# Retention with a gated convolution on one core: the first batch in order of arrival, its queries by chunk, output weights later

## The chip, the core and the metric

The kernel runs on one core of a Trainium2 chip. The metric is the device time of one execution, in microseconds (us), from the first to the last instruction. TensorE (PE) multiplies matrices into PSUM, VectorE (DVE) and ScalarE (ACT) read PSUM and write SBUF, GpSimd (POOL) works on SBUF alone, and SyncE (SP) issues nearly all DMA transfers, in the order of its program. Every engine works through its own list of instructions in order and waits where an instruction needs something that isn't there yet.

## What is computed

Eight batches of 576 tokens go through decayed attention with 8 heads of 64, and the result through a gated block of width 512:

```python
q, k, v: (8, 8, 576, 64) float32        # batch, heads, tokens, head size
scores = scale * q @ k.T                # scale = 1/8
Dmat   = gamma[h] ** (i - j) if i >= j else 0
x      = (scores * Dmat) @ v            # heads side by side: (8, 576, 512)

gate = sigmoid(sum over kk = 0..4 of conv_w[kk] * x[token - 4 + kk])   # causal, per channel
val  = x @ w_val                        # 512 x 512
out  = (gate * val) @ w_out             # 512 x 512, float32
```

There is no softmax. The decay splits into a factor of the query's token (`gout`) and one of the key's token (`gin`), so that only a 0/1 mask stays inside a chunk, and everything before the chunk goes through a state of 64 x 64 for each head, to which each chunk adds k.T @ v.

## The kernel before

Tokens are taken in chunks of 128; batches come in groups of four. Of each group the 16 full chunks come first, and then the last 64 tokens of its batches, two batches to a "tail" chunk: 36 chunks in all, numbered 0 to 35 in this order. Two chunks make a unit, so there are 18 units of convolution, gate, value and output product.

Loads: k and v of a full chunk are 256 KB each, in pieces of 64 floats (256 B). The queries of a batch come as one load of 1 MB, in which a partition takes four neighbouring tokens, so that a piece is 1 KB. The four turns of such a load give queries in an order in which a chunk's columns are interleaved; `mask_q` is the mask in this order, and the convolution's input is written back in the order of tokens.

```python
def load(t):                       # k and v of chunk t, of a tail its q too
    load_one("k", k, kind, b, c, LA + 1)          # LA = 8
    if kind == "tail":
        load_one("q", q, kind, b, c, 2)
    load_one("v", v, kind, b, c, LA + 1)

def load_queries(b):
    t = half.tile([P, H, RQ, D], F32, name="fqb", bufs=2)
    nc.sync.dma_start(out=..., in_=q[b, :, 0:RQ * P, :].rearrange("h (p r) d -> p h (r d)", r=RQ))

load_one("k", k, *chunks[0], LA + 1)
load_queries(0)
load_one("v", v, *chunks[0], LA + 1)
load(1)
...                                # wvf: w_val, one load of 1 MB
load(2)
...                                # wof: w_out, four loads of 64 rows each
load(3)
load_queries(1)
for t in range(4, LA - 2):
    load(t)
```

For each chunk: k, q and v are cast to bf16 (v times `gin`); k and q are transposed on TensorE and copied out of PSUM; scores, the mask, the part carried by the state, the values, the update of the state. The steps of the main loop hold these for several chunks at once:

```python
for t in range(-2, NT + 2):        # NT = 36
    n = t // 2 - 1                 # the unit: convolution and value in an even step, output in the odd one
    ...                            # t == -2: cast and turn chunk 0's k, all of batch 0's q
    for b in qload.get(t, []): load_queries(b)
    load(t + LA - 2)
    cast_v(t + 2); cast_k(t + 3); cast_q(...)
    take_state(t)
    scores(t + 1); masks(t + 1, 0)
    values(t)
    ...
    conv(n); gate(n, 0); gate(n, 1)           # even t
    turn_k(t + 2)
    ...
    project(n, 0) if odd else value(n, 0)
    turn_q(...)
    project(n, 1) if odd else value(n, 1)     # project stores to the output, by SyncE
    carried(t + 1); update(t + 1)
    ...                            # in the first steps: conversion of the weights
```

(Conditions on the range of t are left out.) Each store of the output is an instruction on SyncE, in line with the loads: the stores of unit n come before the load of chunk 2n + 10.

Of the kernel before, what the change touches and what calls it, by code (L numbers as in the profile page):

```python
# [21 lines left out]
def kernel(  # L22
# [48 lines left out]
    with tc.manual_schedule():  # L71
# [13 lines left out]
        def load(t):  # L85
            kind, b, c = chunks[t]
            load_one("k", k, kind, b, c, LA + 1)
            if kind == "tail":
                load_one("q", q, kind, b, c, 2)
            load_one("v", v, kind, b, c, LA + 1)  # L90
# [9 lines left out]
        load_one("k", k, *chunks[0], LA + 1)  # L100
        load_queries(0)
        load_one("v", v, *chunks[0], LA + 1)
        load(1)
        wvf = consts.tile([P, NP, DM], F32, name="wvf")
        wof = consts.tile([P, NP, DM], F32, name="wof")
        nc.sync.dma_start(out=wvf, in_=moe_w_val.rearrange("(o i) n -> i o n", i=P))
        load(2)
        wo_src = moe_w_out.rearrange("(pr ab hl p) n -> ab hl p pr n", pr=2, ab=2, hl=2)
        for (p0, blk, ab, hl) in ((0, 0, 0, 0), (64, 0, 1, 0), (0, 2, 1, 1), (64, 2, 0, 1)):
            nc.sync.dma_start(out=wof[p0:p0 + 64, blk:blk + 2, :], in_=wo_src[ab, hl])  # L110
        load(3)
        load_queries(1)
        for t in range(4, LA - 2):
            load(t)


        lrow = consts.tile([P, H], F32, name="lrow")
# [33 lines left out]
        for pr in range(NP):  # L151
            nc.scalar.activation(gout[:, pr, :], posi, AF.Exp, bias=lsc, scale=lcol[:, pr:pr + 1])

        sbd = [consts.tile([P, NP, P], BF16, name=f"sbd{i}") for i in range(2)]
        sbl = [consts.tile([P, NP, P], BF16, name=f"sbl{i}") for i in range(GB)]
        xg = [xp.tile([P, GB, NP, PAD + S], BF16, name=f"xg{g}") for g in range(B // GB)]
        for t in sbd:
            nc.vector.memset(t, 0.0)
# [30 lines left out]
        def prep_wo(copy, o):  # L189
            copy(wob[:, o], wof[:, o])  # L190
# [4 lines left out]
        def cast_k(t):  # L195
            kb = bfp.tile([P, H, D], BF16, name="kb")
            (nc.vector if t < 2 else nc.gpsimd).tensor_copy(kb, loaded["k", *chunks[t]])  # L197
            kbf[t] = kb
# [47 lines left out]
        def queries(t, rows, pr):  # L246
            kind, b, c = chunks[t]
            if kind == "tail":
                return qtd["own", t][rows, pr, :]
            return qtd["batch", b][rows, pr, :, c * P // RQ:(c + 1) * P // RQ]  # L250
# [15 lines left out]
        def masks(t, i):  # L266
            m = mask_q if chunks[t][0] == "full" else mask_t
            p = pp.tile([P, NP, P], BF16, name=f"p{i}")
            nc.vector.tensor_tensor(p, sps[t][i], m.unsqueeze(1).to_broadcast([P, NP, P]), op=ALU.mult)  # L269
            pt[t, i] = p  # L270
# [33 lines left out]
        def take_x(t):  # L304
# [3 lines left out]
            if kind == "full":  # L308
                i0 = c * P
                by_token = lambda a: a.rearrange("p o (n r) -> p o n r", r=RQ)  # L310
# [94 lines left out]
        qjobs = {1: [], 2: [("batch", 1, r) for r in range(RQ)]}  # L405
# [8 lines left out]
        for b in range(2, B):  # L414
            first = min(s for s in qjobs if ("batch", b, 0) in qjobs[s])
            qload.setdefault(max(0, first - LA + 2), []).append(b)

        v_copy, g_copy, s_copy = nc.vector.tensor_copy, nc.gpsimd.tensor_copy, nc.scalar.copy
        for t in range(-2, NT + 2):
            n = t // 2 - 1  # L420
            unit = 0 <= n < NT // 2
            odd = t % 2 == 1
            jobs = qjobs.get(t, [])
            if t == -2:

                cast_k(0)
                turn_k(0)
                for s in sbl:
                    nc.vector.memset(s, 0.0)
                for r in range(RQ):  # L430
                    cast_q(("batch", 0, r), nc.vector if r % 2 else nc.gpsimd)
                cast_v(0)
                for r in range(RQ):
                    turn_q(("batch", 0, r), s_copy if r % 2 else v_copy, ps_g if r < 3 else None)
                warm = consts.tile([P, 1], F32, name="warm")
                nc.scalar.activation(warm, lsc, AF.Sigmoid)
                continue
            for b in qload.get(t, []):
                load_queries(b)
            if t >= 0 and ok(t + LA - 2):  # L440
                load(t + LA - 2)
            if ok(t + 2) and t == -1:
                cast_k(t + 2)
            if ok(t + 2):
                cast_v(t + 2)
            if t == -1:
                prep_wv(g_copy, 0)
# [4 lines left out]
            if ok(t):  # L452
# [4 lines left out]
            if ok(t):  # L457
# [9 lines left out]
            if ok(t + 2) and not 1 <= t <= 3:  # L467
                turn_k(t + 2)
            if ok(t) and odd:
# [3 lines left out]
            if t == -1:  # L473
                prep_conv_weights()
            early = jobs if not 1 <= t <= 3 else []
            if unit:
                project(n, 0) if odd else value(n, 0)
            for job in early:
# [3 lines left out]
            if ok(t + 2) and 1 <= t <= 3:  # L482
                turn_k(t + 2)
                for i, job in enumerate(jobs):
                    turn_q(job, v_copy if i % 2 else s_copy)
# [3 lines left out]
            if -1 <= t <= 0:  # L489
                prep_diagonals(2 * t + 2)  # L490
                prep_diagonals(2 * t + 3)
            if t == 1:
                prep_wv(s_copy, 1)
            if t == 2:
                for o in range(NP):
                    prep_wo(s_copy if o % 2 else v_copy, o)
                nc.gpsimd.tensor_copy(mask_t, mask)
                nc.gpsimd.memset(mask_t[0:64, 64:128], 0.0)
# [29 lines left out]
```

## Time and profile before

| | before |
|---|---|
| time, median of 3 (lowest, highest) | 177.1 us (176.44, 177.12) |
| profiled span | 177.4 us |
| PE busy | 151.7 us (86%), 2,273 products |
| DVE, ACT, POOL busy | 117.7, 88.4, 81.6 us |
| DMA | 40.20 MB, mean 227 GB/s, 93,958 packets |
| packets under 512 B | 80,090 |

The page divides the span in 40 slices and gives each a digit, the busy share in tenths. It also follows the chain that ended last back from the end, from each instruction to what released it. Two columns of the view by groups matter here: the busy time of a group, and the idle time before it with its releaser. The chunk's number isn't in the trace; it follows from the order, since loads and casts of k run in order of chunks. A DMA's time "to landing" is from its issue to the signal that its data is there, and so holds the time that it stood behind others.

### The profile page before, as it was taken

What the parts mean: (1) busy time and instruction counts of PE and PEld (TensorE: products, weight loads), DVE (VectorE), ACT (ScalarE), POOL (GpSimd) and SP (SyncE); (2) the same over time, 40 slices, a digit from 0 to 9 for tenths busy, and PEclk for the clock granted to TensorE, in tenths of its full rate; (3) what the DMA queues carried; (4) which work ended last, traced back from release to release, by engine and by line L of the source; (5) the groups of instructions that cost most, each with busy time, mean ns of one, the idle gap of its engine ahead of it and who ended that gap; (6) DMA issues with size and microseconds to landing.
All of it is one profiled execution on the core that took longest, in us unless ns stands there. A gap on an engine that the chain in (4) does not pass through costs nothing.

```text
span 177.4 us, 5549 instructions
## 1 busy us (share of the span) xinstructions
PE 151.7 (86%) x2273; PEld 112.2 (63%) x2273; DVE 117.7 (66%) x229; ACT 88.4 (50%) x180; POOL 81.6 (46%) x119
## 2 busy tenths in 40 slices
PE   0166359398999999999999969999999999999980
PEld 0055147247786868677786848686777868677640
DVE  6558724366867777877867747777778678876430
ACT  6351412345565565557554545655575654455231
POOL 5165135492942494631386058524775662620000
PEclk9999999969999999999999999999999999999998
DMA  5999999999999899989999979999989998853114
GB/s 126 292 280 247 220 291 211 296 294 206 266 262 256 207 271 213 251 209 235 249 247 285 287 181 245 292 207 215 288 228 224 276 251 180 203 213 123 51 68 118
DMA packets 93958, 40.20 MB, mean 227 GB/s; under 512 B 80090, under 2 KB 88302, under 8 KB 93934
## 3 DMA queue, kind: packets, MB, share of 16 engines
q1 hardware_dynamic: 93744, 39.59, 90.9%
q8 instruction: 17, 0.28, 0.7%
q10 hardware_dynamic: 190, 0.27, 0.6%
q14 instruction: 7, 0.06, 0.1%
HBM read 30.42 MB, written 9.44 MB: 225 GB/s over the span
## 4 chain that ended last, share of the span: by engine, by line
PE 74%; DMA 9%; SPq 8%; DVE 2%; POOL 2%; ACT 1%; issue 1%; ACTq 0%; DVEq 0%; POOLq 0%
PE g L391 17%; PE g L380 17%; PE g L365 12%; PE tps L222 10%; DMA fkc<-in_k_dram 9%; PE o L301 6%; PE s L260 6%; SPq L78 4%; PE st L332 4%; SPq L110 3%; PE o L284 3%; POOL kb L197 1%; DVE z L383 1%; ACT qtb L244 1%; ACT ob L394 1%
## 5 line engine op out<-in xcount | busy, mean ns | idle before, releaser
L269 DVE TENSOR_TENSOR p<-s,maskq 128x512 bf16<-128x512 f32 x64 | 43.9, 685 | 15.6 <-PE s L260 15.4
L197 POOL CAST kb<-fkc 128x512 bf16<-128x512 f32 x34 | 20.8, 611 | 50.4 <-DMA fkc<-in_k_dram 38.0
L202 POOL TENSOR_TENSOR vb<-fvc,gin 128x512 bf16<-128x512 f32 x36 | 37.6, 1044 | 12.6 <-DMA fvc<-in_v_dram 9.0
L383 DVE TENSOR_TENSOR z<-gate,g 128x512 bf16<-128x512 f32 x36 | 24.8, 688 | 20.4 <-PE g L380 20.4
L391 PE MATMUL g<-wob,z 128*128 128x512 bf16 x144 | 37.5, 389 | 0.3 <-DVE z L383 0.3
L380 PE MATMUL g<-xg,wvb 128*128 128x256 bf16 x288 | 36.9, 274 | 0.0
L394 ACT COPY ob<-g 128x512 f32<-128x512 f32 x36 | 21.1, 586 | 28.9 <-PE g L391 28.6
L373 ACT ACTIVATE gate<-g 128x512 f32<-128x512 f32 x36 | 19.5, 594 | 20.0 <-PE g L365 20.0
L380 PEld LDWEIGHTS <-wvb 128*128 128x128 bf16 x288 | 26.8, 98 | 3.5 <-issue 0.8
L343 ACT CAST sbd<-st 64x256 bf16<-64x256 f32 x48 | 17.6, 366 | 16.2 <-PE st L332 15.7
L222 PE MATMUL tps<-ident,kb 128*128 128x128 bf16 x144 | 15.1, 231 | 12.1 <-POOL kb L197 7.5
L365 PE MATMUL g<-xg,dg 64*64 64x256 bf16 x720 | 24.3, 279 | 0.0
L215 POOL CAST qb<-fqb 128x512 bf16<-128x512 f32 x30 | 18.7, 632 | 7.1 <-DMA fqb<-in_q_dram 7.1
L311 DVE TENSOR_TENSOR xg<-o,gout 128x512 bf16<-128x512 f32 x32 | 21.8, 680 | 0.0
L230 DVE COPY kt<-tps 128x512 bf16<-128x512 bf16 x36 | 15.3, 424 | 8.5 <-PE tps L222 8.2
L365 PEld LDWEIGHTS <-dg 64*64 64x64 bf16 x720 | 19.0, 109 | 2.3 <-issue 0.6
L244 ACT COPY qtb<-tps 128x512 bf16<-128x512 bf16 x27 | 15.9, 589 | 8.7 <-PE tps L222 8.7
L391 PEld LDWEIGHTS <-z 128*128 128x128 bf16 x144 | 12.9, 100 | 11.6 <-issue 1.8
L222 PEld LDWEIGHTS <-kb 128*128 128x128 bf16 x144 | 8.8, 101 | 17.5 <-POOL kb L197 8.6
L222 PEld LDWEIGHTS <-qb 128*128 128x128 bf16 x144 | 11.3, 103 | 11.6 <-POOL qb L215 4.2
L222 PE MATMUL tps<-ident,qb 128*128 128x128 bf16 x132 | 13.0, 222 | 3.3 <-DVE kt L230 1.5
L301 PE MATMUL o<-p,vb 128*64 128x128 bf16 x288 | 15.8, 235 | 0.0
(58 smaller groups left out, 123.2 us busy)
## 6 DMA issues: line engine op xcount, KB each, us to landing
fkc<-in_k_dram SPq DMA_DIRECT2D x32, 256.0 KB, 5.3
fqb<-in_q_dram SPq DMA_DIRECT2D x8, 1024.0 KB, 7.9
fvc<-in_v_dram SPq DMA_DIRECT2D x32, 256.0 KB, 5.7
out_dram<-ob SPq DMA_DIRECT2D x32, 256.0 KB, 4.3
wvf<-in_moe_w_val_dram SPq DMA_DIRECT2D x1, 1024.0 KB, 6.5
wof<-in_moe_w_out_dram SPq DMA_DIRECT2D x4, 256.0 KB, 6.2
fkc<-in_k_dram SPq DMA_DIRECT2D x8, 128.0 KB, 3.9
fqc<-in_q_dram SPq DMA_DIRECT2D x8, 128.0 KB, 4.6
```

Of the source, the lines that this page charges most:

```text
L197: (nc.vector if t < 2 else nc.gpsimd).tensor_copy(kb, loaded["k", *chunks[t]])
L202: nc.gpsimd.tensor_tensor(vb, loaded["v", *chunks[t]], gin[:, chunks[t][2], :].unsqueeze(2).to_broadcast([P, H, D]), op=ALU.mult)
L222: nc.tensor.transpose(ps[:, pr, :], flat[:, pr * P:(pr + 1) * P], ident)
L269: nc.vector.tensor_tensor(p, sps[t][i], m.unsqueeze(1).to_broadcast([P, NP, P]), op=ALU.mult)
L301: nc.tensor.matmul(o[r, pr, :], lhsT=vb[:, 2 * pr + i, :], rhs=pt[t, i][:, pr, :], start=(fresh and pr == 0), stop=(pr == NP - 1), skip_gr ...
L311: nc.vector.tensor_tensor(by_token(x[:, bl, :, PAD + i0:PAD + i0 + P]), ops[t].rearrange("p o (r n) -> p o n r", r=RQ), by_token(gout[:, : ...
L365: nc.tensor.matmul(g[bank][cols, pr, :], lhsT=dg[rows, blk, kk, :], rhs=xs(n, rows, blk, kk), start=(pr == 0 and kk == 0), stop=(pr == 1 a ...
L373: nc.scalar.activation(t, gps[n][i], AF.Sigmoid)
L380: nc.tensor.matmul(vps[:, j, :], lhsT=wvb[:, o, 2 * i + j, :], rhs=xs(n, slice(0, P), o, PAD), start=(j == 0 and o == 0), stop=(j == 1 and ...
L383: nc.vector.tensor_tensor(z, gsb[n][i], vps, op=ALU.mult)
L391: nc.tensor.matmul(o, lhsT=zsb[n, j // 2][:, j % 2, i * P:(i + 1) * P], rhs=wob[:, j, :], start=(j == 0), stop=(j == NP - 1))
L394: nc.scalar.copy(ob, o)
```

## The change

It is meant to let TensorE start in earnest sooner. The parts:

- The first batch is written out by hand, in place of the loop's first steps, in the order in which its loads arrive; the loop starts at t = 3. With it, the first two units' work is placed by hand.
- The queries of batch 0 are loaded by chunk, like k and v, right beside them. They come in order of tokens, so this batch uses the plain mask and writes the convolution's input straight.
- The load of w_out comes after chunk 3 in place of ahead of it, as one load of 128 rows and two of 64. The queries of batch 2 and chunks up to 8 are sent ahead of the loop.
- Products on zeros, which nobody reads, are put in the first waits (`keep_warm`), to keep TensorE's clock up.
- Small things: chunk 2's k is cast by VectorE; the table `gout` is made after chunk 0's queries are turned; the zeros of `sbl` are written by GpSimd.

```diff
@@ loads
-            if kind == "tail":
-                load_one("q", q, kind, b, c, 2)
+            if kind == "tail" or b == 0:
+                load_one("q", q, kind, b, c, NCH)
@@
-        load_one("k", k, *chunks[0], LA + 1)
-        load_queries(0)
-        load_one("v", v, *chunks[0], LA + 1)
+        load(0)
         load(1)
         wvf = consts.tile([P, NP, DM], F32, name="wvf")
-        wof = consts.tile([P, NP, DM], F32, name="wof")
         nc.sync.dma_start(out=wvf, in_=moe_w_val.rearrange("(o i) n -> i o n", i=P))
         load(2)
+        load(3)
+        wof = consts.tile([P, 2, 2, DM], F32, name="wof")
-        for (p0, blk, ab, hl) in ((0, 0, 0, 0), (64, 0, 1, 0), (0, 2, 1, 1), (64, 2, 0, 1)):
-            nc.sync.dma_start(out=wof[p0:p0 + 64, blk:blk + 2, :], in_=wo_src[ab, hl])
-        load(3)
+        nc.sync.dma_start(out=wof[:, 0], in_=moe_w_out.rearrange("(pr ab i) n -> ab i pr n", pr=2, ab=2)[0])
+        nc.sync.dma_start(out=wof[0:64, 1], in_=wo_src[1, 1])
+        nc.sync.dma_start(out=wof[64:128, 1], in_=wo_src[1, 0])
         load_queries(1)
-        for t in range(4, LA - 2):
+        load(4)
+        load(5)
+        load_queries(2)
+        for t in range(6, LA + 1):
             load(t)
@@ masks and the convolution's input
-            m = mask_q if chunks[t][0] == "full" else mask_t
+            m = mask_t if kind == "tail" else mask if b == 0 else mask_q
@@ the schedule
+        idle = ps_g.tile([P, DM], F32, name="g")
+        def keep_warm(n):
+            for _ in range(n):
+                nc.tensor.matmul(idle, lsT0, rhs0, start=True, stop=True)   # zeros, 128x512
-        for t in range(-2, NT + 2):
+        keep_warm(6)
+        cast_k(0)
+        turn_k(0)
+        prep_conv_weights()
+        cast_q(("own", 0))
+        keep_warm(3)
+        turn_q(("own", 0), v_copy)
+        prep_gout()
+        scores(0)
+        cast_v(0)
+        prep_diagonals(0)
+        cast_k(1)
+        keep_warm(3)
+        turn_k(1)
+        ...                      # chunk 0, chunk 1
+        conv(0)
+        gate(0, 0)
+        gate(0, 1)
+        ...                      # value(0), chunk 2, chunk 3, prep_wo
+        conv(1)
+        gate(1, 0)
+        gate(1, 1)
+        value(1, 0)
+        for r in range(RQ):
+            cast_q(("batch", 1, r))
+        value(1, 1)
+        project(0, 0)
+        ...                      # batch 1's queries and chunk 4's k turned
+        for t in range(3, NT + 2):
+            unit = 2 <= n < NT // 2
+            ...                  # as before; project(1) at t == 4
```

## The prediction

> **What bounds the kernel now.** I read the page's strip of the span first, then the chain of waits, then GpSimd's timeline, then the DMA traffic in short windows. The strip makes TensorE look like the bound after a bad start:
>
> ```profile
> PE   0166359398999999999999969999999999999980
> DMA  5999999999999899989999979999989998853114
> ```
>
> TensorE is thin for nine slices of 4.4 us (about 40 us) and full afterwards, which is what the change goes for. But the DMA row is just as full, and from the second slice on. So two things are nearly balanced, and the chain of waits has to say which one rules where. Its columns are start, duration and what ran:
>
> ```profile
> 91.40 0.87 PE g L380 x8
> 92.60 1.06 POOL vb L202
> 93.75 8.95 DMA fkc<-in_k_dram
> 102.82 0.62 POOL kb L197
> 103.49 0.40 PE tps L222 x4
> 103.89 0.86 PE g L391 x4
> ```
>
> In mid-span, long after the start, TensorE stood still for a load of k. Casts of k run in chunk order (chunks 0 and 1 on VectorE, the rest on GpSimd), so the one at 102.82 is chunk 21. After it, the chain is TensorE almost without a break to 177.4. GpSimd's timeline shows which casts came the moment their load landed (the bracket is idle time and its releaser):
>
> ```profile
> 83.19 0.61 POOL L197 CAST kb<-fkc 128x512 bf16<-128x512 f32 x1 [3.97 <-DMA fkc<-in_k_dram]
> 89.11 0.61 POOL L197 CAST kb<-fkc 128x512 bf16<-128x512 f32 x1 [1.14 <-DMA fkc<-in_k_dram]
> ...
> 102.82 0.61 POOL L197 CAST kb<-fkc 128x512 bf16<-128x512 f32 x1 [5.62 <-DMA fkc<-in_k_dram]
> ...
> 123.23 0.61 POOL L197 CAST kb<-fkc 128x512 bf16<-128x512 f32 x1 [2.25 <-DMA fkc<-in_k_dram]
> ...
> 130.03 0.61 POOL L197 CAST kb<-fkc 128x512 bf16<-128x512 f32 x1 [1.25 <-DMA fkc<-in_k_dram]
> ```
>
> These are chunks 17, 18, 21, 26 and 28. Setting each cast's end beside the start of the transposes of the same k in the chain gives the slack of the load: chunk 10, 51.7 against 59.4, 7.6 us; chunk 16, 75.4 against 83.2, 7.9; chunk 17, 83.8 against 86.7, 2.9; chunk 18, 89.7 against 91.1, 1.4; chunk 21, none; chunk 26, 123.8 against 124.2, 0.3; chunk 28, 130.6 against 132.0, 1.3; chunk 34, 149.2 against 155.2, 6.0. So up to chunk 21 the DMA runs down TensorE's slack, and from there to the end TensorE is the bound with 177.4 - 103.5 = 73.9 us of its own work ahead.
>
> **What the Trainium skill says.** "Perfetto Trace Analysis", section "What 'DMA-bound' means": look whether the engines or the issuing sequencer is solid. In this trace SyncE's issues follow one another from 0.8 to 153 us. "DMA: Bandwidth & Descriptors", sections "Specifications" and "Why small descriptors are slow": pieces below 512 B do not reach line rate. The trace agrees; these are two 4 us windows of its DMA view, 52 to 56 us (a third of the packets are 1 KB pieces of q) and 60 to 64 us (k and v alone, 256 B):
>
> ```profile
> DMA packets 2426, 1.24 MB, mean 309 GB/s; under 512 B 1615, under 2 KB 2426, under 8 KB 2426
> ...
> DMA packets 3310, 0.85 MB, mean 212 GB/s; under 512 B 3302, under 2 KB 3302, under 8 KB 3310
> ```
>
> "TensorE: Matmul & The Clock Gate", part "The HAM clock gate", says the clock is halved after an idle window of about 3.4 us and comes back after one of steady work. The trace agrees: the granted clock is 0.66 between 35 and 40 us, and eight 512-column products there take 3.07 us where later sets of four take 0.86.
>
> **The change part by part.**
>
> *The hand order of the first batch.* Before, SyncE sends all of batch 0's q (1 MB) ahead of the first v, and both weights (2 MB) before chunk 3: chunk 3's k is issued at 16.3 and cast at 23.41, and TensorE stands 4.87 us for it. Now each chunk's k, q, v come together (0.79 MB), wv after two chunks, wo after four. The third unit's convolution starts at 50.31 in the chain before; in both programs the same work precedes it, so it is the marker for how much the start gains. That convolution stands in step 6, behind the transposes of chunk 7's k. That k was cast at 43.30, on landing. In the new order the fourth batch-load of q, 1 MB, no longer goes ahead of it (about 3 us earlier at 309 GB/s), against the cost worked out next (1.5 us later). So k of chunk 7 comes near 42, and with 1.5 to 2 us of TensorE work the convolution starts near 44: TensorE is about 6 us ahead of before. The lead can't be more, whatever the hand order saves earlier, since that load stands in its way.
>
> *The q loads by chunk.* Same bytes, but 4 x 1,024 pieces of 256 B in place of 1,024 pieces of 1 KB. By the windows: 1.05 MB at 212 GB/s is 4.9 us; at 309 GB/s 3.4 us, and less for the 1 KB pieces alone, whose share of that window must have run faster than its mean. DMA time goes up by 1.5 to 2.4 us. For wo, half now goes in full 128-row form in place of 64-row pieces; the window from 16 to 20 us, mostly wo, moved 226 GB/s against 263 over 4 to 56 us, so half a megabyte gets about 0.3 to 0.7 us cheaper. Net about +1.5 us on everything that lands after it, chunk 21 included. From chunk 9's load on, the sequence of loads and stores is as before, so nothing else makes chunk 21's load earlier by order.
>
> *What TensorE's lead gives back to the DMA.* SyncE is in order, so a store waiting for its tile holds back loads. Before, the second unit's stores held it 2.0 us near 55, and the window 56 to 60 has a DMA share of 0.67: 0.33 x 4 = 1.3 us idle. With a 6 us lead these tiles are ready. Later waits of 0.7 to 0.8 us for stores (64 to 96 us) are mostly covered by queued transfers; I allow 0.3. Return: about 1.6 us by chunk 21. From 4 to 56 us the mean is 263 GB/s with no hole in the busy row, so there is nothing to win there.
>
> *Products on zeros.* Twelve 512-column products; at the cold pace of 3.07/8 they are 4.6 us in waits for the first loads. They only matter to a stage that the DMA overtakes later. Likewise the moved casts, gout and the masks.
>
> *Sum.* Chunk 21's k lands at 102.8 + 1.5 - 1.6 = 102.7, plus 0.7 for cast and start, plus 73.9 us of unchanged TensorE work: 177.3 by this profile, 177.0 by the median before. The 6 us lead is spent between chunks 17 and 21 as waits for k.
>
> **The rivals.** *TensorE bounds it from 40 us on and the lead stays.* For it: 20.00 us of 20 busy from 60 to 100 us and 120 to 160. Against it: slack of 0 at chunk 21 and 0.3 at chunk 26, with GpSimd idle 38.0 us in all for k. It would give 177 - 6 = 171. *The DMA gets more back than I count*, because every store is ready and the queue never thins: the share falls to 0.8 to 0.9 in windows at 72 to 80, 88 to 92 and 100 to 108. That would be 2 to 3 us: 174 to 175. Against it: no wait of SyncE at all stands in 72 to 88. *It gets slower*: the small pieces cost the full 2.4 us with little given back, and TensorE, now waiting 3 to 5 us at a time before chunks 17 to 21, is granted half clock as it was at 36 to 40 us, just when it becomes the bound. A cold spell at the rate of 3.07 against 1.73 costs about 1.3 to 1.7 us. Then 179 to 180.
>
> **Range and chances.** The central sum is a difference of two terms of 1.5 us, each good to 1 us, and the cold spell adds on the slow side: 174.8 to 179.2 should hold 8 times in 10. Faster by over 2% (below 173.6) needs the first rival in part, or the second in full: 0.12. Slower by over 2% (above 180.6) needs all of the third: 0.06. Within 2%: 0.82.
>
> **What would show it.** Right: the third unit's convolution starts at 42 to 46 us; GpSimd's wait for k in the page grows beyond 38 us; TensorE has new waits of 1 to 5 us between 60 and 105 us; chunk 21's k (the 19th such cast on GpSimd now, since three run on VectorE) is cast within 2 us of 102.8; after it, about 74 us without waits; pieces under 512 B rise by about 4,096 from 80,090. Wrong: if the convolution comes at 40 or sooner, if the lead is still there at chunk 21 because its load lands at 98 or before, or if TensorE waits at chunks 26 and 28 more than at 21. The first two would mean that the DMA was not at its limit in mid-span, and the time would fall with them.

## The result, and the profile after

| | before | after |
|---|---|---|
| time, median of 4 | 176.97 us (176.44 to 177.12) | 179.62 us (178.64 to 182.84) |
| ratio, 95% interval | 1 | 1.0137 [1.0088, 1.0185] |
| profiled span | 177.4 us | 177.8 us |
| third unit's convolution starts | 50.24 us | 50.33 us |
| TensorE waits for k after it | 1.4 us | 1.9 us |

The kernel became 1.4% slower, where 177.0 us and a range up to 179.2 had been predicted. One thing is needed to read times and spans: both profiled executions of the kernel before (177.4 us above, 176.2 us in the run e0 below) were disturbed or long ones, 79 undisturbed executions of it beside the experiments have a median span of 175.2 us, e16's profile was of a disturbed execution too and isn't used, and the medians of the table of runs below leave disturbed executions out. An execution's time is usually 2.0 us more than its span in the kernel before, and 1.7 us in the changed one.

The strip of the page after (TensorE's busy share, its granted clock, the DMA, 40 slices of 4.4 us):

```profile
PE   6767759958899999999979989999999999999980
PEclk9985985885899999999999999999999999999997
DMA  6999997999989899989899999999999988863124
```

and the clock row of the kernel before:

```profile
PEclk9999999969999999999999999999999999999998
```

TensorE is busier in the first ten slices than before (6767759958 against 0166359398), in part with products on zeros, in part because it works at half clock: that comes and goes up to 46 us. The row of before looks better than it was. Its trace holds no clock entry ahead of 29.3 us, and the view fills in full clock there; but TensorE's products ran at half pace up to that point (the last section has the lines). So half clock in the start isn't new.

GpSimd's casts of k that came just as their load landed, after; these are chunks 18, 21 and 25:

```profile
91.44 0.61 POOL L207 CAST kb<-fkc 128x512 bf16<-128x512 f32 x1 [2.89 <-DMA fkc<-in_k_dram]
...
103.25 0.61 POOL L207 CAST kb<-fkc 128x512 bf16<-128x512 f32 x1 [4.12 <-DMA fkc<-in_k_dram]
...
119.41 0.61 POOL L207 CAST kb<-fkc 128x512 bf16<-128x512 f32 x1 [4.18 <-DMA fkc<-in_k_dram]
```

Its total wait for k, from the view of waits (us in total, times, longest):

```profile
POOL kb L207 <- DMA fkc<-in_k_dram: 41.4, 18, 6.3
```

and the packets:

```profile
DMA packets 97063, 40.22 MB, mean 226 GB/s; under 512 B 84218, under 2 KB 91406, under 8 KB 97038
```

Chunk 21's k is cast at 103.25, 0.4 us later than in the first profile of before, and the wait for k is 3.4 us longer (2.1 us longer than in e0). Packets under 512 B rise by 4,128, where about 4,096 were expected. All this is as predicted. What isn't: the convolution of the third unit, TensorE's own timeline after (start, duration, line):

```profile
47.57 0.40 PE L232 MATMUL tps<-ident,kb 128*128 128x128 bf16 x4
...
50.33 1.29 PE L379 MATMUL g<-xg,dg 64*64 64x256 bf16 x40
```

The first of these lines turns chunk 7's k, the load that was to set the start. GpSimd had cast that k long before, without a wait for its load:

```profile
40.58 0.61 POOL L207 CAST kb<-fkc 128x512 bf16<-128x512 f32 x1
```

So the k lay there for 6.4 us (41.2 to 47.6). TensorE was late. Its waits between 9 us and the convolution, after:

```profile
PE s L270 <- ACT qt L254: 2.0, 2, 1.3
PE tps L232 <- DVE kt L240: 1.6, 3, 0.6
PE o L312 <- DVE p L280: 1.5, 5, 0.4
PE g L379 <- DVE xg L322: 1.5, 2, 1.2
```

and before:

```profile
PE tps L222 <- POOL kb L197: 6.1, 2, 4.9
PE g L222 <- POOL qb L215: 4.0, 1, 4.0
```

Before, three waits for data to be loaded and cast make 10.1 of 14.7 us. After, there are nineteen waits, 9.8 us in all, nearly all of them short, each for a neighbour's answer to a product just made: the turned k or q copied out of PSUM, the mask, the convolution's input. But for 0.6 us on a cast of q the loads are gone from the list, and the convolution comes no sooner.

### The profile page after: what moved, and what is told of

Its sections match the earlier page's. It is cut to its first block, busy times and chain, and to the rows that moved or that the text cites. A ratio compares the mean times of both kernels' runs of the same rounds, so it can differ in the third digit from the quotient of the medians.

```text
span 177.8 us, 5555 instructions
## 1 busy us (share of the span) xinstructions
PE 157.3 (88%) x2267; PEld 115.0 (65%) x2285; DVE 116.2 (65%) x223; ACT 89.9 (51%) x181; POOL 83.9 (47%) x124
## 4 chain that ended last, share of the span: by engine, by line
PE 62%; DVE 14%; DMA 12%; ACT 3%; issue 3%; SPq 1%; POOL 1%; ACTq 0%; DVEq 0%; POOLq 0%
PE g L394 15%; PE g L405 14%; DMA fkc<-in_k_dram 12%; PE g L379 12%; PE tps L232 8%; DVE p L280 6%; PE s L270 4%; PE o L312 4%; DVE z L397 4%; PE st L346 2%; PE o L295 1%; DVE kt L240 1%; DVE xg L322 1%; POOL kb L207 1%; ACT qt L254 1%
## 5 line engine op out<-in xcount | busy, mean ns | idle before, releaser
L280 DVE TENSOR_TENSOR p<-s,maskq 128x512 bf16<-128x512 f32 x56 | 38.4, 686 | 16.6 <-PE s L270 16.4
L207 POOL CAST kb<-fkc 128x512 bf16<-128x512 f32 x33 | 20.1, 610 | 45.7 <-DMA fkc<-in_k_dram 41.4
L394 PE MATMUL g<-xg,wvb 128*128 128x256 bf16 x288 | 38.2, 280 | 0.0
L405 PE MATMUL g<-wob,z 128*128 128x512 bf16 x126 | 34.1, 388 | 1.5 <-DVE z L397 0.5
L379 PE MATMUL g<-xg,dg 64*64 64x256 bf16 x720 | 25.4, 287 | 1.5 <-DVE xg L322 1.5
L379 PEld LDWEIGHTS <-dg 64*64 64x64 bf16 x720 | 20.4, 112 | 3.5 <-issue 2.2
L225 POOL CAST qb<-fqb 128x512 bf16<-128x512 f32 x28 | 17.0, 613 | 8.1 <-DMA fqb<-in_q_dram 8.1
L254 ACT COPY qtb<-tps 128x512 bf16<-128x512 bf16 x26 | 15.3, 588 | 10.8 <-PE tps L232 10.8
L325 DVE TENSOR_TENSOR xg<-o,gout 128x512 bf16<-128x512 f32 x28 | 19.1, 680 | 0.0
L232 PE MATMUL tps<-ident,qb 128*128 128x128 bf16 x144 | 14.4, 224 | 3.0 <-DVE kt L240 1.6
```

Source lines behind the costliest of these rows:

```text
L207: (nc.vector if t < 3 else nc.gpsimd).tensor_copy(kb, loaded["k", *chunks[t]])
L232: nc.tensor.transpose(ps[:, pr, :], flat[:, pr * P:(pr + 1) * P], ident)
L325: nc.vector.tensor_tensor(by_token(x[:, bl, :, PAD + i0:PAD + i0 + P]), ops[t].rearrange("p o (r n) -> p o n r", r=RQ), by_token(gout[:, : ...
L379: nc.tensor.matmul(g[bank][cols, pr, :], lhsT=dg[rows, blk, kk, :], rhs=xs(n, rows, blk, kk), start=(pr == 0 and kk == 0), stop=(pr == 1 a ...
L394: nc.tensor.matmul(vps[:, j, :], lhsT=wvb[:, o, 2 * i + j, :], rhs=xs(n, slice(0, P), o, PAD), start=(j == 0 and o == 0), stop=(j == 1 and ...
L405: nc.tensor.matmul(o, lhsT=zsb[n, j // 2][:, j % 2, i * P:(i + 1) * P], rhs=wob[:, j, :], start=(j == 0), stop=(j == NP - 1))
```

## The experiments

The theories, as they stood when the runs began and were refined:

- The DMA sets the arrival of k in mid-span, so that any lead of TensorE is spent as waits there. The small pieces make it land later.
- The start of the hand-written version isn't set by loads any more, but by its chain from one engine to the next, and by half clock in it (the expectations from e8 on call this and the first point together C).
- The loss is the hand order itself, against the loop's.
- Later: what limits k in mid-span is the one queue that issues all loads, not the 16 DMA engines.

What each run gave, first in one table. "Start" is the start of the third unit's convolution; "waits" are TensorE's waits for k after it; the last column is the span less both. Times are medians; start, waits and span are of the one profiled execution.

| run | time us | ratio to before [95%] | start | waits | span | rest |
|---|---|---|---|---|---|---|
| after | 179.62 | 1.0137 [1.0088, 1.0185] | 50.33 | 1.9 | 177.8 | 125.6 |
| e0 before again | 178.03 | 1.0051 [1.0017, 1.0085] | 49.34 | 1.1 | 176.2 | 125.8 |
| e1 | 179.06 | 1.0079 [1.0041, 1.0117] | 49.15 | 1.8 | 177.1 | 126.2 |
| e2 | 179.88 | 1.0124 [1.0089, 1.0158] | 50.12 | 1.0 | 176.7 | 125.6 |
| e3 | 181.11 | 1.0227 [1.0145, 1.0310] | 50.12 | 2.2 | 178.0 | 125.7 |
| e4 | 182.71 | 1.0303 [1.0229, 1.0377] | 55.22 | 0 | 180.8 | 125.6 |
| e5 | 179.60 | 1.0153 [1.0069, 1.0237] | 51.98 | 0 | 177.4 | 125.4 |
| e6 | 181.89 | 1.0257 [1.0180, 1.0333] | 54.78 | 0 | 180.5 | 125.7 |
| e7 | 195.54 | 1.1013 [1.0932, 1.1094] | | | 193.9 | |
| e8 | 180.37 | 1.0166 [1.0084, 1.0248] | 51.57 | 0 | 177.3 | 125.7 |
| e9 | 172.95 | 0.9762 [0.9683, 0.9842] | 45.33 | 0 | 170.9 | 125.6 |
| e10 | 178.78 | 1.0080 [1.0041, 1.0120] | 51.66 | 0 | 177.2 | 125.5 |
| e11 | 177.44 | 1.0009 [0.9971, 1.0047] | 48.45 | 1.7 | 176.0 | 125.9 |
| e12 | 179.34 | 1.0162 [1.0073, 1.0251] | 51.35 | 0.7 | 177.7 | 125.7 |
| e13 | 178.60 | 1.0127 [1.0048, 1.0207] | 49.48 | 0.9 | 176.1 | 125.7 |
| e14 | 180.16 | 1.0205 [1.0127, 1.0284] | 47.64 | 4.4 | 177.9 | 125.9 |
| e15 | 179.95 | 1.0104 [1.0060, 1.0149] | 49.19 | 0 | 178.0 | 128.8 |
| e16 | 180.01 | 1.0110 [1.0079, 1.0140] | | | | |
| e17 | 179.39 | 1.0111 [1.0074, 1.0149] | 50.65 | 0 | 177.5 | 126.9 |

The last column is the finding of the whole study: 125.4 to 126.2 us in all kernels whose loads SyncE alone issues from mid-span on, and also in e6. From the third convolution on TensorE's work is one flat block. The span is that block, plus when it starts, plus its waits for k.

**e0, the kernel before once more.** No edit.

> The kernel before, unchanged, for a second profile of it: its first profile had a span of 177.4 us, while the times of the kernel before and after differ from their spans by 1.8 us, so a typical span of before should be 175.2 us. Both theories expect 177 us and a span near 175.3; the wait for chunk 21's k should be shorter than the 1.4 us of the first profile.

Its ratio to itself is 1.0051, with an interval that doesn't hold 1. So half a per cent isn't resolved here, and differences below about 0.9% aren't read as such. What TensorE waited for k after the third convolution (us in total, times, longest):

```profile
PE tps L222 <- POOL kb L197: 1.1, 2, 0.8
```

Chunk 21's k was cast at 101.38 in this execution, against 102.82 in the profile that the prediction read: the load's hour moves by more than 1 us from one execution to the next.

**e1, the small pieces alone.** The kernel before, with batch 0's queries in four loads of 256 B pieces.

```diff
-            nc.sync.dma_start(out=<all of t>, in_=<1 KB pieces of q[b]>)
+            if b == 0:
+                for r in range(RQ):
+                    nc.sync.dma_start(out=t[:, :, r, :], in_=<256 B pieces, turn r>)
```

> The kernel before with one thing changed: batch 0's queries, same tile and same order, come as four loads of 1,024 pieces of 256 B in place of one load of 1,024 pieces of 1 KB. Theory A (the small pieces cost DMA time, which nothing gives back, and set the end): 1.5 to 2.4 us slower, 178.5 to 179.4. Theory B (the rest of the change makes it slower: the clock in the hand-written start, or the order of loads): within 0.5 us of before.

The third convolution starts as in e0 (49.15 against 49.34). The k of chunks 9 to 12 come 1.3 to 2.7 us later than in e0, and 1.8 to 3.3 us later than in the first profile of before. Chunk 21's comes 1.0 us later than in e0 (102.37), but 0.4 us sooner than in the first profile. TensorE waits 1.8 us for k in place of 1.1, with 0.9 us more of span. In time it is 1.0 us above e0 in the median, between the two theories, which the intervals don't separate. So the small pieces delay the early chunks; the size of their term at chunk 21, estimated at 1.5 us, isn't resolved.

**e2, no products on zeros.** The changed kernel without its twelve.

```diff
-        keep_warm(6)
-        keep_warm(3)
-        keep_warm(3)
```

> The changed kernel without its twelve products on zeros. Theory A: within 0.7 us of the changed kernel (179.6), since the start doesn't set the end. Theory B with the clock as cause: the granted clock is worse in the first 10 us and the time 1 us or more longer than the changed kernel's.

Start 50.12, time 179.88: no difference from after. The twelve do act on the clock: in after it is full from 4.8 to 11.6 us, without them TensorE runs at half pace up to 21.3 us. But after that half clock comes back three times in after, 20.5 us in all, and in e2 twice, 6.8 us in all. By the third convolution the twelve don't matter, as the prediction had said.

**e3, 39 more of them, all through the start.** A tile of zeros of its own, and between the steps of chunks 0 to 3:

```diff
+        def fill(n):
+            g = ps_g.tile([P, DM], F32, name="g")
+            for _ in range(n):
+                nc.tensor.matmul(g, zeros, zeros_512, start=True, stop=True)
+        fill(2)                  # and so on, up to 5 at a place
```

> The changed kernel with 38 more products on zeros, put ahead of the products that wait in the hand-written part, so that TensorE is busy in the windows after which its clock was halved (16 to 20, 24 to 32 and 40 to 48 us). All theories: fewer halved windows, and the third unit's convolution starts at 44 to 47 us in place of 50.4. Theory A: the lead is spent on waits for k until chunk 21, time 178.0 to 179.6. Theory B (clock): the lead lasts, time 174 to 177.

The clock is full from 12.5 us on, and from the first to the third convolution it now takes 31.8 us in place of 35.5: the half clock costs the start about 3.7 us there. But the first convolution starts at 18.30 in place of 14.79, since the first products on zeros wait for their tile and run cold, ahead of the work. The third starts at 50.12 as before. Gain and cost cancel. (Its four executions fall in two pairs, near 179.8 and 182.4 us; the profile is of the first, and the gap isn't explained.) This run doesn't yet show what a lead is worth.

**e4, the hand order with one large load of q.** As the kernel before has it, 1 MB, ahead of the first v.

```diff
-        load(0)
+        load_one("k", k, *chunks[0], LA + 1)
+        load_queries(0)
+        load_one("v", v, *chunks[0], LA + 1)
```

> The changed kernel with batch 0's queries as one load of 1 KB pieces again, and the rest of the hand order kept. Theory A (the small pieces are DMA time that delays every later k, and the hand order brings no lead): k of chunks 21 to 26 is cast 1 to 1.5 us earlier than in the changed kernel (102.0, 118.2 and 122.5 for 21, 25 and 26), time 0.7 to 1.5 us less than the changed kernel's, near the kernel before. Theory B (the order of loads or of the hand-written work costs): no gain, 179 to 180.

Neither expectation held. The start is at 55.22, 4.9 us later than after, and k is never waited for. In the hand order the queries by chunk are worth 5 us of start, although they cost the DMA time.

**e5, batch 1's queries and chunk 4 ahead of the output weights.**

```diff
+        load_queries(1)
+        load(4)
         wof = consts.tile([P, 2, 2, DM], F32, name="wof")
...
-        load_queries(1)
-        load(4)
```

(with it, the casts of w_out and the first output products were placed later.)

> The changed kernel with w_out loaded after batch 1's queries and chunk 4, and with chunk 4's turns ahead of the first output product, which moves into the loop's first step. Theory A: batch 1's queries, landed at 28.6 us, are what holds the third unit's convolution at 50.3; now they land 3 us earlier and the convolution starts at 46 to 48, but k still comes when the DMA brings it, so that the time stays within 1 us of the changed kernel (178.6 to 180.6). Rival (the start sets the end): the time falls by as much as the convolution moves, to 176 or 177.

Chunk 4's k was cast at 26.7 us in place of 31.9, and turned at 35.6 us, where after has 36.0. The third convolution came at 51.98, not at 46 to 48. A load 5 us earlier moved nothing: what stood in the way was TensorE's own row. The time is that of after.

**e6 and e7, all loads of v issued by ScalarE**, in the kernel before (e6) and in the changed one (e7).

```diff
+            queue = nc.scalar if name == "v" else nc.sync
-                nc.sync.dma_start(out=t, in_=src[b, :, c * P:(c + 1) * P, :]...)
+                queue.dma_start(out=t, in_=src[b, :, c * P:(c + 1) * P, :]...)
```

> The kernel before with all loads of v issued by ScalarE, and nothing else changed. Theory A1 (the 16 DMA engines are full): k of chunk 21 is cast within 1 us of before (101.4 to 102.8), time within 1 us of 177.5 or slower for the issue time on ScalarE. Theory A2 (SyncE's issuing is the limit with loads of 256 B pieces): chunk 21's k comes 3 us or more earlier, TensorE doesn't wait for k after 50 us, time 173 to 176.

> The changed kernel with all loads of v issued by ScalarE. Theory A1: within 1 us of the changed kernel (178.6 to 180.6). Theory A2: loads at the start come earlier, batch 1's queries before 26 us, and the time is 174 to 177.

e6 starts 5.4 us late (54.78): ScalarE has v's loads in line with its own work at the start, and six of their issues take it 15.0 us ahead of that work. But from there on k is never waited for, chunk 21's is there at 100.6 in spite of the late start, and between 86 and 114 us the DMA moved 307 GB/s, against 257 in the same stretch of e0. e7 is 10% slower. ScalarE's loads of v at its start (start, duration), and its longest wait:

```profile
1.49 18.17 ACTq L79 DMA_DIRECT2D fvc<-in_v_dram  x9
```

```profile
ACT L151 <- DMA fvc<-in_v_dram: 19.7, 1, 19.7
```

Nine issues of about 2 us each stand ahead of ScalarE's first own work, the table `gin`. Without `gin` GpSimd can't cast v, and TensorE waits 11.6 us at once for it. e6 gave the idea for e15; e7 shows why that can go wrong.

**e8 and e9, without the weights' loads**, 2 MB: in the changed kernel (e8) and the kernel before (e9). w_val and w_out are constants here, so the output is that of constant weights.

```diff
-        nc.sync.dma_start(out=wvf, in_=moe_w_val...)
-        nc.sync.dma_start(out=wof..., in_=...)        # all of w_out
+        nc.gpsimd.memset(wvb, 0.01)
+        nc.gpsimd.memset(wob, 0.01)
```

> The changed kernel without the loads of the two weights (2 MB, both are constants of 0.01 written in SBUF; the output is that of constant weights). Theory C (the hand-written part is set by its own chain of TensorE, VectorE and ScalarE, and the end is the later of that start plus 125.5 us of TensorE work, and of k's landing): the third unit's convolution moves by less than 2 us, to 48.5 to 50.5; no waits for k after it; span 174 to 176, time 176 to 178. Theory D (loads set the hand-written part): the convolution 4 to 7 us earlier, time 171 to 174.

> The kernel before without the loads of the weights, in the same way. Its start waits for chunk 3's k behind the weights, so k of chunk 3 comes 6 us earlier and the third unit's convolution starts at 43 to 46 in place of 49.3 to 50.3; no waits for k after it; time 170 to 173. If its start is a chain of engines like that of the changed kernel, the convolution stays above 47.

This pair separates the theories of the start. The third convolution without weights, in the changed kernel (e8):

```profile
51.57 1.29 PE L373 MATMUL g<-xg,dg 64*64 64x256 bf16 x40
```

and in the kernel before (e9):

```profile
45.33 1.29 PE L360 MATMUL g<-xg,dg 64*64 64x256 bf16 x40
```

The kernel before starts 4.0 us sooner than in e0 once 2 MB are out of the way: its start is set by loads. The hand-written start doesn't move (51.57 against 50.33, if anything later), though the loads land far sooner (chunk 21's k is cast at 98.8 us in place of 103.25). Its waits between 9 and 51.5 us are the same short ones, with nearly the same sums, and none is for a load or for GpSimd, which now writes the constants:

```profile
PE s L264 <- ACT qt L248: 2.0, 2, 1.3
PE g L373 <- DVE xg L316: 1.7, 2, 1.4
PE tps L226 <- DVE kt L234: 1.6, 3, 0.6
```

From its first convolution (16.70) to its third it takes 34.9 us, where after takes 35.5.

e9 shows one thing more. There chunk 21's k is cast at 92.9, no k is waited for, and 4.0 us of start are worth 4.3 us against the usual span (170.9 against 175.2): a lead is worth its full time where k comes in time.

**e10, the changed kernel without the stores of units 0 to 4.** That part of the output isn't written.

```diff
+                if n < 5:
+                    return
```

> The changed kernel without the stores of the first five units (2.5 MB of output left unwritten, all computing kept). Theory C: the third unit's convolution as before at 50.3, no waits for k behind it, span 175.8 to 176.3, time 177.5 to 178.2, which is the DMA's part of the loss: 1.5 to 2 us under the changed kernel. If DMA has no part in it: 179.6 as the changed kernel.

Chunk 21's k comes at 95.8, 7.4 us sooner than in after, and TensorE no longer waits for k at all. Yet the span is 177.2, since the third convolution starts at 51.66, where 50.3 was expected. So with the waits taken out of after, 2.0 of the 2.6 us of span lost to the usual 175.2 are still there, by the ratios 0.8 of 1.4%, with intervals that overlap: most of the loss is in the start.

**e11, the output weights later, alone.** The kernel before, w_out behind chunk 3, batch 1's queries and chunk 4.

```diff
         load(2)
-        <four loads of w_out>
         load(3)
         load_queries(1)
-        for t in range(4, LA - 2):
-            load(t)
+        load(4)
+        <four loads of w_out>
+        load(5)
```

> The kernel before with one part of the change alone: w_out's four loads come after batch 1's queries and chunk 4. Chunk 3's k comes 4 us earlier. Theory C: the third unit's convolution starts 0 to 3 us earlier, k of chunks 17 to 26 comes as before, and TensorE waits the difference there: time within 1 us of the kernel before. Rival (the start alone sets the end): 174 to 176.

Start 48.45, 0.9 us sooner than e0; 1.7 us of waits for k after it, 0.6 more; the time is the same as before (ratio 1.0009). Most of the 0.9 us went as waits, as far as single profiles can show so small a difference.

**e12 and e13, the loop's order with the changed loads.** e12 has the queries by chunk and the order of the first loads of the changed kernel (w_out after chunk 3, then batch 1's queries, then chunk 4), but the loop's own steps. e13 is e12 with batch 0's queries in two loads of 512 KB, pieces of 512 B.

```diff
-        load_one("k", k, *chunks[0], LA + 1)
-        load_queries(0)
-        load_one("v", v, *chunks[0], LA + 1)
+        load(0)                  # k, q, v of a chunk together
...
-        qjobs = {1: [], 2: [...]}
+        qjobs = {-1: [("own", 1)], 0: [("own", 2)], 1: [("own", 3)], 2: [...]}
```

> The kernel before in its loop's order, with the changed loads alone: batch 0's queries by chunk beside k and v, w_out after chunk 3. Theory C (the hand order costs the start, the small pieces delay k, the end is the later of the two): chunk 3's k comes 3 to 5 us earlier than before, the third unit's convolution starts at 45 to 48.5, and the lead is spent on 2 to 4 us of waits for k at chunks 17 to 26; span 176.5 to 177.5, time 178 to 179.3. If the loads alone brought the loss through the start: the convolution at 50 or later. If the start alone set the end: 174 to 176.

> As e12, but batch 0's queries come as two loads of 512 KB in pieces of 512 B, for chunks 0 and 1 and for chunks 2 and 3. Theory C: the third unit's convolution at 46 to 49, k of chunks 21 to 26 as in the kernel before or up to 0.5 us later, time within 1 us of the kernel before, between it and e12.

e12's third convolution comes at 51.35, not at 45 to 48.5. Here it is loads: TensorE waits 5.2 us for chunk 4's k, which stands behind w_out and batch 1's queries. Its time is 179.34, that of after. So the hand order as such isn't the loss: with the same queries by chunk, the loop's order is as slow, for another reason. e13 is 0.7 us below e12, with intervals that overlap; 512 B pieces aren't shown to be better.

**e14, zeros only where they cost nothing.** The changed kernel with 28 more products on zeros, but from chunk 2's queries on, behind the first convolution.

```diff
+        fill(2)                  # eleven such places between chunk 2's queries and batch 1's last queries
```

> The changed kernel with 28 more products on zeros, only from chunk 2's queries on (e3 also had them before, and started 3.5 us later for it). Clock full in most of 20 to 50 us. Theory C: the third unit's convolution at 46.5 to 48.5 in place of 50.3, k as in the changed kernel, 3 to 5 us of waits for k behind it, span 177 to 178, time within 0.8 us of the changed kernel (179.6). If the start alone set the end: 176 to 177.5.

This is the one kernel with the lead that the change was to bring. The granted clock and the rest of the stretch from 8 to 48 us, in after and in e14 (window, length, busy time of PE, PEld, DVE, ACT, POOL with the instructions, granted clock, DMA share, GB/s):

```profile
8.00:48.00 40.00, 30.70 (x329) 21.62 (x329) 21.13 (x38) 15.73 (x31) 22.22 (x33) 0.74 1.12 259
```

```profile
8.00:48.00 40.00, 32.35 (x405) 21.20 (x412) 23.71 (x44) 17.16 (x34) 21.90 (x33) 1.00 1.13 262
```

The clock was at 0.74 in after, and is full in e14 from 9.8 us on. (In e14's three other executions the mean clock is 0.971 to 0.984, against 0.998 in this one, so that they had some half clock again.) The third convolution:

```profile
47.64 1.29 PE L381 MATMUL g<-xg,dg 64*64 64x256 bf16 x40
```

That is 2.7 us sooner than in after. What TensorE then waits for between 45 us and the end:

```profile
PE tps L234 <- POOL kb L209: 4.4, 6, 1.2
```

and chunk 21's k, on GpSimd:

```profile
102.46 0.61 POOL L209 CAST kb<-fkc 128x512 bf16<-128x512 f32 x1 [2.94 <-DMA fkc<-in_k_dram]
```

Of 2.7 us of lead, 2.5 went as more waits for k (4.4 against 1.9), and the span is 177.9 against 177.8. Chunk 21's k came 0.8 us sooner, which may be what a lead gives back to the DMA, though that load moves by more than 1 us between executions. This is the prediction's step of the spent lead, seen with a lead that is there. It isn't spent quite where the prediction had it: a first 0.95 us goes at chunk 11, and 1.0 us at chunks 25 and 26, after chunk 21.

**e15, e16 and e17, v from a second queue in mid-span.** ScalarE issues the loads of v from the loop's fourth step on in the kernel before (e15) and in e11's (e17), from the loop's first step on in e14's (e16).

```diff
+            queue = nc.scalar if name == "v" and in_loop else nc.sync
...
+            if t == 3:
+                in_loop.append(1)
```

> The kernel before, with the loads of v issued by ScalarE instead of SyncE from the loop's fourth step on (the loads of the start stay as they are). Theory (one issuing queue, and not the 16 DMA engines, limits k in mid-span): the third unit's convolution stays at 49.3 us, TensorE's waits for k after it go from 1.1 us to 0-0.2, chunk 21's k is cast before 99 us instead of 101.4, and the span is 49.3 + 125.7 = 175.0 us, the time 0.5 to 1.5 us below the kernel before. Rival (the DMA engines are the limit, or the issues hold up ScalarE): chunk 21's k no earlier than 101, span 176 or more, time the same or longer.

> The kernel of e14 (changed kernel with 28 more products on zeros from chunk 2's q on) with v issued by ScalarE from the loop's first step on. Theory: the start stays at 47.6 us, the 4.4 us of waits for k fall below 1 us, and the span is 47.6 + 125.7 = 173.3 to 174.3 us; the time 175 to 176.5, about 4 us below e14 and 1 to 2 below the kernel before: the lead is worth its full time once k comes in time. Rival: waits of 3 us or more stay, and the time stays near 180.

> The kernel of e11 (kernel before with the output weights later) with v issued by ScalarE from the loop's fourth step on. Theory: the convolution at 48.5 us as in e11, waits for k of 1.7 us fall to 0-0.2, span 48.5 + 125.7 = 174.2, time 175.0 to 176.5, below e15 by about 0.8. Rival: span 176 or more, time within 0.5% of the kernel before.

Half of this held. The DMA between 86 and 114 us, in e0:

```profile
DMA packets 17050, 7.19 MB, mean 257 GB/s; under 512 B 14358, under 2 KB 16272, under 8 KB 17046
```

and in e15:

```profile
DMA packets 19660, 8.45 MB, mean 302 GB/s; under 512 B 16552, under 2 KB 18600, under 8 KB 19654
```

Chunk 21's k in e15 comes at 97.0 in place of 101.4:

```profile
97.03 0.61 POOL L200 CAST kb<-fkc 128x512 bf16<-128x512 f32 x1 [3.03 <-DMA fkc<-in_k_dram]
```

and TensorE waits for no k from the third convolution on, in e15 and e17. But the time isn't less. In e15 TensorE waits for something else from 45 us on:

```profile
PE g L383 <- ACT gate L376: 1.6, 2, 1.2
```

ScalarE's timeline there shows why:

```profile
48.17 0.59 ACT L397 COPY ob<-g 128x512 f32<-128x512 f32 x1
51.23 0.37 ACTq L81 DMA_DIRECT2D fvc<-in_v_dram  x1
51.70 0.76 ACT L346 CAST sbd<-st 64x256 bf16<-64x256 f32 x2 [2.94 <-PE g L383]
52.48 1.09 ACT L376 ACTIVATE gate<-g 128x512 f32<-128x512 f32 x2
```

Between its copy at 48.17 and the issue at 51.23 it does nothing. The view puts the idle time down to a product, but the state that it casts next was ready at 49 us (e0 casts it at 48.83). Ahead of that cast stands a load of v that isn't issued until 51.23. Its buffer isn't the reason: this is chunk 12's v, and the cast that frees its buffer, of chunk 3's v, ended at 24.3 us. The order is shown; what held the issue is open. The cast comes 2.9 us late, the gate with it, and TensorE waits. In e17 the same kind of wait, 3.1 us for the gate, lies ahead of the third convolution and makes it 50.65. So one wait took the place of another. e15 loses 0.5 us more on TensorE than it gains, and the last store ends 1.3 us later after its copy than in e0, which isn't explained; nor are 1.2 us of e17's last column. e16 has a ratio of 1.011 where e14 has 1.0205, with intervals that just overlap; a part of its gain may be real, but the 4 us that were expected aren't there.

## Why the prediction was wrong

**What held.** The small pieces rose by 4,128. GpSimd's wait for k grew to 41.4 us. Chunk 21's k came within 0.5 us of the cast time that was read for before (1.9 us after e0's). After it came the same flat work: its cast starts at 103.25, and the span ends 74.5 us later, with one more wait for k in it, 0.2 us for chunk 25. The products on zeros didn't matter (e2). A lead is spent as waits for k (e14, and e11 within its small size).

**The step that failed** is the convolution "near 44", with its reason: "The lead can't be more, whatever the hand order saves earlier, since that load stands in its way." The load of chunk 7's k was taken as the only limit of the start. The limit on it was even estimated on the safe side, since that k was there at 40.6, not at 42. But TensorE came to it only at 47.6, and to the convolution at 50.33: no lead, in place of 6 us. The hand order moved TensorE's start from waits for loads, some 10 us, to a chain in which it makes one small set of products, waits about half a microsecond for VectorE or ScalarE to bring it out of PSUM, and makes the next, with half clock for 20 of its first 46 us. Such waits (9.8 us between 9 and 50.3) and the half clock weren't in the sum at all, although the kernel before had run at half pace up to 29 us too. e8 shows that loads don't set this start, e5 that an earlier load doesn't move it, e3 and e14 that the clock is worth 2.7 to 3.7 us of it. The rest, the chain's own waits, follows from the list of waits; no run takes them out. With no lead there were no "new waits of 1 to 5 us between 60 and 105 us" either: after has two there, of 0.95 and 0.69 us. A convolution that comes late was not among the prediction's signs of being wrong.

"The Trainium skill" is right here where the prediction didn't follow it far enough: "TensorE: Matmul & The Clock Gate", "Part 1: The HAM clock gate", ties the clock to TensorE's recent activity. The third rival did count a cold spell of 1.3 to 1.7 us, but put it at chunks 17 to 21, where after has full clock (1.00 from 45.7 us to the end of TensorE's work). So its 179 to 180 us is close to the 179.62 measured by luck. Half clock belonged to the start, where TensorE's work is a row of short sets with gaps. Nor did the half clock at 36 to 40 us agree with an idle window, as the prediction read it: in the 6.8 us ahead of it TensorE's longest wait is 1.0 us.

**The terms of the sum.** For small pieces 1.5 us were put in; for chunk 21, e1 has 1.0 more than one profile of before and 0.4 less than the other. Their rate was read from a window with 256 B pieces alone, 212 GB/s; that isn't the pieces' own limit, since in e15, with v from a second queue, 4 us with 96% such packets (96 to 100 us) moved 279 GB/s. For what a lead gives back, 1.6 us from 6 us of lead; e14 has 0.8 from 2.7, about the same rate, from single executions. But after has no lead, so the term is zero: with it gone, the prediction's own sum reads 177.0 + 1.6 = 178.6. Measured were 179.62.

**The remaining 1.0 us** isn't settled. One part is how the base was read. The slack table came from one long execution, with 1.4 us of waits for k. In the usual execution of before the span is 175.2, so start and waits together are 175.2 - 125.7 = 49.5 us. With starts at 49.2 to 50.2 in the profiles, little or no wait for k is left in it: start and k are level there, where the prediction had k come last by a clear margin. For after the same sum is 177.8 - 125.7 = 52.1 us, 50.3 of start and 1.9 of waits, and its usual span is the profiled one. That says where the 2.6 us are, in the start and in the waits, but not how they split in an execution of before that no profile shows.

Why the two only come together as a loss is seen from e10 and e14. Take the waits for k away (e10), and the start sets the end. Make the start early (e14), and k sets it. The change had moved neither: it replaced one limit of the start by another of the same length, and it loaded the DMA a little more.

## What to carry to other kernels

Before an order is changed to bring loads sooner, lay out the chain that remains when all loads are there, with each hand-over between engines (about half a microsecond here) and with the half clock that TensorE had in such a chain here; the later of the two sets the start. Where a kernel's front end and its loads are level, as here, a gain on one alone is returned by the other: look for the block of flat work, and sum start, waits and block for each variant. A second queue for loads helps only on an engine whose own work can stand behind the issues of these loads (18.2 us for nine of them in e7).

## What the runs showed of the hardware

A second issuing queue was worth more than expected. "The Trainium skill", "DMA: Bandwidth & Descriptors", section "Issuing engines are not separate DMA queues", says that issuing from several engines saves only the sequencer's time, usually little. Here v from ScalarE's queue raised the rate between 86 and 114 us from 257 to 302 GB/s (e15 against e0), with the same size of pieces, and brought chunk 21's k 4.4 us sooner. The sequencer's time wasn't small here: SyncE's issues fill 26.8 of these 28 us in e0, and 20.0 in e15. Whether the gain is that time, or that v no longer stands behind stores and other loads in SyncE's line, wasn't separated.

A granted clock of 1.00 in a view can mean that the trace has no entry yet. The first entries are at 29.3 us in the first profile of before, 28.2 in e0, 4.8 in after, 21.3 in e2. Ahead of them the products themselves show half pace. The first and the second convolution of the kernel before, in e0, the same 40 products:

```profile
26.27 2.18 PE L365 MATMUL g<-xg,dg 64*64 64x256 bf16 x40
41.30 1.29 PE L365 MATMUL g<-xg,dg 64*64 64x256 bf16 x40
```

and in after the second one, in a stretch that its trace does give as half clock:

```profile
28.11 2.35 PE L379 MATMUL g<-xg,dg 64*64 64x256 bf16 x40 [0.24 <-DVE xg L322]
```

Half clock came without an idle window. After its first entry, the clock of after is halved at 11.6 to 18.4, 25.3 to 32.1 and 38.9 to 45.7 us, each time for 6.8 us, with full clock between. In each 6.8 us of full clock ahead of a halving TensorE was busy for 4.3 to 4.5 us, and its longest wait was 1.3 us. Two windows at the second halving:

```profile
24.00:28.00 4.00, 2.33 (x24) 1.63 (x24) 1.93 (x4) 0.95 (x3) 0.00 (x0) 0.66 1.07 285
28.00:32.00 4.00, 3.89 (x48) 3.08 (x48) 1.25 (x3) 3.76 (x6) 2.38 (x5) 0.50 0.63 140
```

Which measure of activity rules it isn't shown. That 28 products on zeros between the work can hold it at full clock, is (e14: 1.00 from 9.8 us to the end of the start).
